# Banks, buffers and ranks: late units of w3 @ w_out in the transposes' banks, score banks kept by the two-branch block, logits behind the first expert product

## The chip, the cores and the metric

The kernel runs on one core of one Trainium2 chip. The metric is the device time of one execution in microseconds (us), as the median of repeated runs. TensorE (PE) does the matmuls and transposes, VectorE (DVE), ScalarE (ACT) and GpSimd (POOL) the element-wise work, and the queue of SyncE (SP) issues almost all DMAs. Each engine takes its instructions in the order of its own program.

## The reference, cut to what matters

```
# 1. attention, 2 batches x 8 heads, 576 positions, head size 64, rotary q and k
attn = softmax(rotate(q) @ rotate(k).T / 8);  x = (attn @ v) laid out as 1152 x 512
# 2. two-branch block
h = ((x @ w1) * (x @ w2)) @ w3                # w1, w2: 512 x 1024, w3: 1024 x 1024
x = h @ w_out                                 # w_out: 1024 x 512
# 3. eight experts, mixed by a gate that is normalised 8 times over rows and columns
P = sinkhorn(exp(x @ w_gate - max))           # 1152 x 8
out = sum_e P[:, e] * (relu(x @ w1e[e]) @ w2e[e])
```

All arrays come as 32-bit or 64-bit floats. Every product is made of three matmuls on pairs (high part, low part) of 32-bit numbers.

## The kernel before, in words

**Stage 1, attention.** The 8 pairs of heads (index n) are worked off tile by tile: five query tiles a pair, the fifth a mixed one. For a tile, PE makes scores into a two-bank PSUM tile of the pool psS (two slots); DVE takes the row maxima (row_max, L371); ACT takes the exponentials (L375); PE transposes them into banks of psT (two slots, L389); ACT or DVE moves them to SBUF (L408); PE multiplies with v into the one bank of psX (values, L446). Keys and queries are rotated on POOL or DVE and spread by DMAs from SBUF to SBUF (kk and sq, L302 to L312).

**Beside it, w3 @ w_out.** The block's last two matrices are multiplied with each other first (w34, 8 row units i). Their 64-bit words come in through two slots of a tile called wide and are turned into a high and a low part by a chain (wide_parts, L174): ACT scales (cvy, L184), DVE shifts, signs and joins in the buffer cvu (L189, L192, L197; two buffers), ACT rounds the high part (L202), POOL or DVE subtracts to get the low part (L205). A unit i takes two pieces u = 2i, 2i+1 of w3, each with four products of three matmuls on all 512 columns (L232 to L234), into one bank; then ACT and DVE split the sum (w34_hi L239, w34_lo L244). w3 has two slots for its pieces, so that piece u+2 is written once the products of u are through. The one bank of psW serves units 0 to 5, a psT bank unit 6 (LATE = 6), and unit 7 (NEARLY) is computed after the stage.

**The order of stage 1 is written out by a planner** (class Plan, L53). Every step has a cost on its engine, the steps that it needs, the slots that it takes and frees, and a rank; whenever an engine is free the step with the lowest rank that can start is next. SIGNAL holds the assumed time from the end of a step to its use on another engine; for a DMA (sp) it is 2.0 beside the time of moving. Where the plan has PE idle before the first step of w34, small matmuls on the identity fill the gap (L623). Ranks of pair n start from t = 18 n: scores at r = t + 3.6 i + j, row_max at r + 0.3, transposes at r + 3.6, values 3.4 tiles after the normalisation's rank; piece u of w3 has 50 + 4.5 u. The products of w34 have ranks above 1000: they run when nothing else can.

**Stage 2, the two-branch block.** Here and later the compiler's scheduler orders the instructions. The pools psS, psT, psX and psW are closed together, and a pool ps of eight banks is opened (four called u, four called z; L629 to L631). Unit 7 of w34 comes first. Then for each of 8 blocks f (columns of w1 and w2, two pieces each through the same wide_parts chain, w12_unit) four branches run, 320, 256, 320 and 256 tokens wide: 12 matmuls into bank pa, 12 into pb (three, L146 to L148), ACT copies pa (a, L664), DVE multiplies it with pb (gf, L666), ACT and DVE split the result (L140, L141). Below, branch k is the k-th of the 32; f = k // 4. merge then multiplies with w34, 4 products a call, in banks u (k = 0) or z (k = 1).

**Stage 3, gate and experts.** All eight banks change hands again (pool pp). logits makes x @ w_gate for the two halves of the tokens (L883), then the experts' products run to the end (hidden, project), with PE almost without a gap.

Of the kernel before, what the change touches and what calls it, by code (L numbers as in the profile page):

```python
# [10 lines left out]
F32 = mybir.dt.float32  # L11
# [7 lines left out]
P = 128  # L19
# [22 lines left out]
WU = 512  # L42
NEARLY = 7
LATE = 6
NSTEP = 2 * E
# [7 lines left out]
class Plan:  # L53
# [4 lines left out]

    SIGNAL = dict(pe=0.28, act=0.14, dve=0.1, pool=0.12, sp=2.0)

# [61 lines left out]
def attention_two_moes(ctx: ExitStack, tc: tile.TileContext, rope, qk, v, mw12, mw3t, mwo, wg, ew1, ew2, out):  # L122
# [20 lines left out]
    def three(ps, terms):  # L143
# [14 lines left out]
    att_p = att.enter_context(sb("att"))  # L158
    psS, psT, psX, psW = (
        aps.enter_context(tc.tile_pool(name=n, bufs=k, space=PSUM)) for n, k in (("psS", 2), ("psT", 2), ("psX", 1), ("psW", 1))  # L160
    )
# [12 lines left out]
    def wide_parts(t, h, l):  # L174

        low, high = t[:, :, 0], t[:, :, 1]
        y = u = None

        def scaled():
            nonlocal y
            y = cv_p.tile([P, WU], F32, name="cvy", bufs=2)
            act.activation(y, f32(high), AF.Copy, scale=2.0**-112)  # L184

        def low_bits():
            nonlocal u
            u = cv_p.tile([P, WU], I32, name="cvu", bufs=2)
            dve.tensor_scalar(u, low, 29, None, op0=ALU.logical_shift_right)  # L189

        def signed():
            dve.scalar_tensor_tensor(  # L192
                out=u, in0=high, scalar=-(2**31), in1=u, op0=ALU.bitwise_and, op1=ALU.bitwise_or
            )

        def joined():
            dve.scalar_tensor_tensor(  # L197
                out=u, in0=y.bitcast(I32), scalar=3, in1=u, op0=ALU.logical_shift_left, op1=ALU.bitwise_or
            )

        def hi_part():
            act.copy(h, f32(u))  # L202

        def lo_part(eng=pool):
            eng.tensor_sub(l, f32(u), f32(h))  # L205

        return scaled, low_bits, signed, joined, hi_part, lo_part
# [17 lines left out]
    def w34_product(u, j, ps_pool, name):  # L225

        i, k = u // 2, u % 2 * 4 + j
        if k == 0:
            w34[i] = ps_pool.tile([P, DM], F32, name=name)
        (h, l, _), (oh, ol, _) = w3[u], wo[k]  # L230
        c = slice(j * P, (j + 1) * P)
        pe.matmul(w34[i], h[:, c], oh, start=(k == 0), stop=False)  # L232
        pe.matmul(w34[i], h[:, c], ol, start=False, stop=False)
        pe.matmul(w34[i], l[:, c], oh, start=False, stop=(k == KF - 1))  # L234
# [184 lines left out]
    def norm_spread(n, g):  # L419

        k = 4 + g
        st["rb", n, g] = rb = att_p.tile([P, 5, D], F32, name="rb", bufs=2)
        act.copy(rb[:, :k], st["sm", n, g][:, :k].unsqueeze(2).to_broadcast([P, k, D]))
# [46 lines left out]

    plan = Plan(psW=1, psX=1, psS=2, psT=2, wide=2, cvy=2, cvu=2, w3=2, raw=2, sq=2, kk=2, v=2, e=2, nm=4, sm=3, rb=2, et0=1, et1=1, r=2, xs=1)

# [14 lines left out]
    for n in range(NP):  # L487
# [33 lines left out]
        for i in range(NQ):  # L521
            g, k, _ = group(i)
            r = t + i * TILE
            for j in range(2 - (i == MIX)):
# [15 lines left out]
                before = [made]  # L540
                step(row_max, (n, i, j), {"dve": 0.68}, r + 0.3, before)
                fr = [("psS", (n, i, j))] + [("nm", (n, i))] * (j or i == MIX)
                step(exponentials, (n, i, j), {"act": 0.73}, r, [(row_max, n, i, j)], frees=fr)
            r += TILE
            parts = 3 - (i == MIX)
# [6 lines left out]
        for g, tiles in enumerate(TILES):  # L552
# [7 lines left out]
            step(norm_moved, a, {"act": act_ps(ng)}, r, [(norm_columns, *a)], [("r", a)], [("psT", (*a, "r"))])  # L560
            r += 3.4 * TILE
            for m, blocks in enumerate(VPARTS):
# [30 lines left out]
    for u in range(2 * KF):  # L593
        i = u // 2
        wide_steps(w3_load, u, w3, 50.0 + 4.5 * u, [("w3", u)])
        if i == NEARLY:
            continue
        for j in range(4):
            needs = [(wo_load, u % 2 * 4 + j, 5), (w3_load, u, 5)]
            needs += [(w34_product, u, j - 1)] if j else [(w34_product, u - 1, 3)] if u else []  # L600
            bank = "psT" if i >= LATE else "psW"
            place = (psT, "t") if i >= LATE else (psW, "w34")
# [26 lines left out]
    aps.close()  # L629
    ps_x = ExitStack()  # L630
    ps_p = ps_x.enter_context(tc.tile_pool(name="ps", bufs=4, space=PSUM))  # L631
# [22 lines left out]
    def branch(f, b, c):  # L654
        wh, wl = w12[f]
        n = CN[c]
        ts = slice(c * CN[0], c * CN[0] + n)
        pa = ps_p.tile([P, 512], F32, name="u")
        pb = ps_p.tile([P, 512], F32, name="u")
        for i, ps in enumerate((pa, pb)):  # L660
# [11 lines left out]
    def merge(c, k):  # L672
# [5 lines left out]
        def product(i, b):  # L678
            ps[i, b] = t = ps_p.tile([P, 512], F32, name="uz"[k])
            ds = slice((2 * i + k) * P, (2 * i + k + 1) * P)  # L680
            bs = slice(b * n, (b + 1) * n)
            three(t[:, :n], [(w34[f][0][:, ds], w34[f][1][:, ds], G[c][:, f, 0, bs], G[c][:, f, 1, bs]) for f in range(KF)])
            return t[:, :n]
# [62 lines left out]
    for u in (2 * NEARLY, 2 * NEARLY + 1):  # L746
        for j in range(4):
            w34_product(u, j, ps_p, "u")
    w34_hi(NEARLY)
# [164 lines left out]
    logits(0)  # L914
    logits(1)
    for k, (c, u) in enumerate(((0, 0), (1, 0), (0, 1), (1, 1))):
        for i, _ in enumerate(hidden(0, c, u)):
            if i == 2 and k == 0:
                gate_start()
# [95 lines left out]
```

## Time and profile before

| | us |
|---|---|
| median of 3 runs (lowest to highest) | 1167.29 (1166.98 to 1168.81) |
| the profiled execution | 1167.42 |
| its span, first to last instruction | 1165.1 |
| PE busy | 1138.6 (98%) |
| DVE busy | 717.8 (62%) |
| ACT busy | 425.5 (37%) |
| POOL busy | 207.3 (18%) |
| mean granted TensorE clock | 0.995 of full speed |

A matmul's row shows a duration that overlaps the next one's, so that the distance between starts is the measure of its cost. "Idle before" is the time in which the engine stood still ahead of an instruction, and the arrow names what ended it. The stages end at about 204 us (attention), 340 us (branches), 391 us (merges).

### The profile page before, as it was taken

The page shows a single profiled execution, that of the slowest core. Times are in us where ns is not written, and L with a number is a line of the kernel's source. Part 1 is how long each engine was busy: PE and PEld are TensorE (multiplying, and loading weights), DVE is VectorE, ACT ScalarE, POOL GpSimd, SP SyncE. Part 2 cuts the span into 40 slices and gives each one's busy share as a digit, 9 for nine tenths or more (in the row PEclk, how much of TensorE's full clock was granted, in tenths as well). Part 3 has the DMA queues.
Part 4 walks back from the last instruction along what each step waited for, and adds up shares of the span by engine and source line. Part 5 has one row for each costly group of instructions (what it writes and reads, how often), then busy time and mean ns, then how long its engine had stood idle before and what let it go on. Part 6 is the DMA issues. An engine that isn't in the chain of part 4 may idle for free.

```text
span 1165.1 us, 17715 instructions
## 1 busy us (share of the span) xinstructions
PE 1138.6 (98%) x7072; PEld 1010.2 (87%) x7072; DVE 717.8 (62%) x1327; ACT 425.5 (37%) x909; POOL 207.3 (18%) x207
## 2 busy tenths in 40 slices
PE   9999999899999999999999999999999999999998
PEld 7867767689999889889889898898988989889887
DVE  6777886796333595565656556566655565655643
ACT  5767666454332343222323232232322232232311
POOL 4475431242000010110211202012011121110200
PEclk9989999999999999999999999999999999999999
DMA  6767771452100021110211101111111111110102
GB/s 214 215 192 211 189 188 37 139 165 78 37 19 1 19 73 37 37 54 20 73 37 37 55 24 68 37 37 55 39 53 39 35 58 52 37 55 19 37 10 73
DMA packets 29153, 83.07 MB, mean 71 GB/s; under 512 B 4880, under 2 KB 6416, under 8 KB 29072
## 3 DMA queue, kind: packets, MB, share of 16 engines
q1 hardware_dynamic: 28528, 81.36, 22.4%
q8 instruction: 55, 0.90, 0.3%
q10 hardware_dynamic: 544, 0.59, 0.2%
q14 instruction: 26, 0.21, 0.1%
HBM read 67.19 MB, written 2.36 MB: 60 GB/s over the span
## 4 chain that ended last, share of the span: by engine, by line
PE 86%; DVE 6%; DMA 3%; ACT 1%; issue 1%; POOL 1%; SPq 1%; DVEq 0%; POOLq 0%; ACTq 0%
PE z L846 12%; PE z L845 11%; PE z L847 11%; PE T L804 4%; PE T L805 4%; PE T L806 4%; PE u L146 3%; PE u L148 3%; PE u L147 3%; PE Q L806 3%; PE Q L804 3%; PE Q L805 3%; PE A L806 3%; PE A L805 3%; PE A L804 3%; PE x L446 2%
## 5 line engine op out<-in xcount | busy, mean ns | idle before, releaser
L847 PE MATMUL z<-w,h 128*128 128x512 f32 x576 | 226.3, 393 | 0.0
L854 DVE SCALAR_TENSOR_TENSOR acc<-z,pr,acc 128x512 f32<-128x512 f32 x135 | 100.9, 748 | 56.6 <-PE z L847 56.5
L847 PEld LDWEIGHTS z<-w,h 128*128 128x128 f32 x576 | 108.0, 187 | 25.3 <-DVE h L811 0.2
L846 PE MATMUL z<-w,y 128*128 128x512 f32 x320 | 126.4, 395 | 0.0
L845 PE MATMUL z<-w,y 128*128 128x512 f32 x320 | 126.3, 395 | 0.0
L724 POOL TENSOR_TENSOR sums<-wide 128x256 f32<-128x256 f32 x28 | 23.7, 848 | 574.5 <-DVE w L141 359.8
L846 PE MATMUL z<-w,h 128*128 128x512 f32 x256 | 101.6, 397 | 0.0
L845 PE MATMUL z<-w,h 128*128 128x512 f32 x256 | 100.8, 394 | 0.0
L140 ACT CAST w<-wide 128x768 fp32r<-128x768 f32 (+1 forms) x64 | 60.4, 943 | 93.2 <-PE z L846 65.0
L810 ACT ACTIVATE y<-tmp 128x320 fp32r<-128x320 f32 x96 | 45.2, 470 | 113.8 <-DVE tmp L826 62.2
L810 ACT ACTIVATE h<-tmp 128x256 fp32r<-128x256 f32 x96 | 40.0, 416 | 127.4 <-DVE tmp L826 120.8
L141 DVE TENSOR_TENSOR w<-wide,w 128x768 fp32r<-128x768 f32 (+1 forms) x64 | 69.6, 1088 | 26.5 <-PE T L806 14.8
L146 PE MATMUL u<-x,w 128*128 128x320 f32 (+1 forms) x256 | 76.4, 298 | 2.6 <-DVE gf L666 2.4
L148 PE MATMUL u<-x,w 128*128 128x320 f32 (+1 forms) x256 | 75.7, 296 | 0.0
L147 PE MATMUL u<-x,w 128*128 128x320 f32 (+1 forms) x256 | 75.4, 295 | 0.0
L846 PEld LDWEIGHTS z<-w,y 128*128 128x128 f32 x320 | 60.7, 190 | 5.7
L845 PEld LDWEIGHTS z<-w,y 128*128 128x128 f32 x320 | 60.2, 188 | 6.0
L811 DVE SCALAR_TENSOR_TENSOR h<-tmp,y 128x320 fp32r<-128x320 f32 x96 | 47.4, 494 | 26.0 <-ACT y L810 25.8
L375 ACT ACTIVATE e<-s,nm 128x576 f32<-128x576 f32 x72 | 53.3, 742 | 18.4 <-DVE nm L371 17.9
L804 PE MATMUL T<-x,w 128*128 128x320 f32 x192 | 59.9, 312 | 0.0
L805 PE MATMUL T<-x,w 128*128 128x320 f32 x192 | 59.2, 309 | 0.0
L806 PE MATMUL T<-x,w 128*128 128x320 f32 x192 | 59.0, 308 | 0.0
(225 smaller groups left out, 3009.5 us busy)
## 6 DMA issues: line engine op xcount, KB each, us to landing
wide<-in_ew_dram SPq DMA_DIRECT2D x64, 512.0 KB, 3.5
wide<-in_mw3t_dram SPq DMA_DIRECT2D x16, 512.0 KB, 4.4
wide<-in_mw_dram SPq DMA_DIRECT2D x16, 512.0 KB, 3.6
raw<-in_qk_dram SPq DMA_DIRECT2D x14, 576.0 KB, 5.4
kk<-raw SPq DMA_DIRECT2D x56, 144.0 KB, 3.1
wide<-in_mwo_dram SPq DMA_DIRECT2D x8, 512.0 KB, 6.7
v<-in_v_dram SPq DMA_DIRECT2D x8, 320.0 KB, 4.1
out_dram<-acc SPq DMA_DIRECT2D x8, 256.0 KB, 2.0
```

Of the source, the lines that this page charges most:

```text
L141: dve.tensor_sub(lo, src, f32(hi))
L146: pe.matmul(ps, wh, xh, start=(i == 0), stop=False)
L147: pe.matmul(ps, wh, xl, start=False, stop=False)
L148: pe.matmul(ps, wl, xh, start=False, stop=(i == n - 1))
L804: pe.matmul(ps, h[:, ws], x[0], start=(first and k == 0), stop=False, **kw)
L805: pe.matmul(ps, h[:, ws], x[1], start=False, stop=False, **kw)
L806: pe.matmul(ps, l[:, ws], x[0], start=False, stop=(k == 1), **kw)
L810: act.activation(h, src, AF.Relu)
L845: pe.matmul(ps, hh[:, f, ts], wh, start=(f == 0), stop=False)
L846: pe.matmul(ps, hh[:, f, ts], wl, start=False, stop=False)
L847: pe.matmul(ps, hl[:, f, ts], wh, start=False, stop=(f == FT - 1))
L854: dve.scalar_tensor_tensor(out=acc[t], in0=ps, scalar=p, in1=acc[t], op0=ALU.mult, op1=ALU.add)
```

## The change

LATE becomes 5: units 5 and 6 of w34 are accumulated in the two psT banks, and unit 5 only starts behind the last transposes of the last pair. psS isn't closed with the other attention pools but lives to the end of stage 2; unit 7 and the branches take its two-bank tiles, pa and pb as the halves of one tile, and so do the products of merge with k = 0 (two pairs a call). The pool ps keeps the four z banks. The conversion buffer cvu has three buffers in place of two; rb, the spread row sums, one in place of two. In the planner: the assumed signal time of a DMA goes from 2.0 to 2.6, row_max from r + 0.3 to r - 0.1, transposes from r + 3.6 to r + 6.0, values from 3.4 to 1.1 tiles behind, piece u of w3 from 50 + 4.5 u to 50 + 7.8 u. In stage 3 logits(1) is issued behind the first product of hidden(0, 0, 0).

```diff
--- before.py
+++ after.py
@@ -41,7 +41,7 @@
 NTT = NT // P
 WU = 512
 NEARLY = 7
-LATE = 6
+LATE = 5
 NSTEP = 2 * E
 FT = F // 2 // P
 
@@ -56,7 +56,7 @@
 
 
 
-    SIGNAL = dict(pe=0.28, act=0.14, dve=0.1, pool=0.12, sp=2.0)
+    SIGNAL = dict(pe=0.28, act=0.14, dve=0.1, pool=0.12, sp=2.6)
 
     SLACK = 0.15
 
@@ -156,8 +156,10 @@
     cv_p = blk.enter_context(sb("cv", side="right"))
     aps, att = ExitStack(), ExitStack()
     att_p = att.enter_context(sb("att"))
-    psS, psT, psX, psW = (
-        aps.enter_context(tc.tile_pool(name=n, bufs=k, space=PSUM)) for n, k in (("psS", 2), ("psT", 2), ("psX", 1), ("psW", 1))
+    ps_x = ExitStack()
+    psS = ps_x.enter_context(tc.tile_pool(name="psS", bufs=2, space=PSUM))
+    psT, psX, psW = (
+        aps.enter_context(tc.tile_pool(name=n, bufs=k, space=PSUM)) for n, k in (("psT", 2), ("psX", 1), ("psW", 1))
     )
 
     YW = 2 * KF * CB[1]
@@ -185,7 +187,7 @@
 
         def low_bits():
             nonlocal u
-            u = cv_p.tile([P, WU], I32, name="cvu", bufs=2)
+            u = cv_p.tile([P, WU], I32, name="cvu", bufs=3)
             dve.tensor_scalar(u, low, 29, None, op0=ALU.logical_shift_right)
 
         def signed():
@@ -226,7 +228,8 @@
 
         i, k = u // 2, u % 2 * 4 + j
         if k == 0:
-            w34[i] = ps_pool.tile([P, DM], F32, name=name)
+            t = ps_pool.tile([P, 2, 512] if name == "s" else [P, 512], F32, name=name)
+            w34[i] = t[:, 0] if name == "s" else t
         (h, l, _), (oh, ol, _) = w3[u], wo[k]
         c = slice(j * P, (j + 1) * P)
         pe.matmul(w34[i], h[:, c], oh, start=(k == 0), stop=False)
@@ -419,7 +422,7 @@
     def norm_spread(n, g):
 
         k = 4 + g
-        st["rb", n, g] = rb = att_p.tile([P, 5, D], F32, name="rb", bufs=2)
+        st["rb", n, g] = rb = att_p.tile([P, 5, D], F32, name="rb", bufs=1)
         act.copy(rb[:, :k], st["sm", n, g][:, :k].unsqueeze(2).to_broadcast([P, k, D]))
 
     def norm_columns(n, g):
@@ -468,7 +471,7 @@
         x, h, l = x_parts(n, g)
         eng.tensor_sub(l, x, f32(h))
 
-    plan = Plan(psW=1, psX=1, psS=2, psT=2, wide=2, cvy=2, cvu=2, w3=2, raw=2, sq=2, kk=2, v=2, e=2, nm=4, sm=3, rb=2, et0=1, et1=1, r=2, xs=1)
+    plan = Plan(psW=1, psX=1, psS=2, psT=2, wide=2, cvy=2, cvu=3, w3=2, raw=2, sq=2, kk=2, v=2, e=2, nm=4, sm=3, rb=1, et0=1, et1=1, r=2, xs=1)
 
     def step(f, args, costs, rank, needs=(), takes=(), frees=(), **kw):
 
@@ -538,10 +541,10 @@
                         needs = needs + [(mix_first, 0), (mix_first, 1)]
                     step(mixed_scores, (n,), {"pe": 1.14 if n else 1.7}, r + j, needs, tk, fr)
                 before = [made]
-                step(row_max, (n, i, j), {"dve": 0.68}, r + 0.3, before)
+                step(row_max, (n, i, j), {"dve": 0.68}, r - 0.1, before)
                 fr = [("psS", (n, i, j))] + [("nm", (n, i))] * (j or i == MIX)
                 step(exponentials, (n, i, j), {"act": 0.73}, r, [(row_max, n, i, j)], frees=fr)
-            r += TILE
+            r += 6.0
             parts = 3 - (i == MIX)
             for p in range(parts):
                 needs = [(exponentials, n, i, min(p, 1) * (i < MIX))] + ([(transposes, n, i, p - 1)] if p else [(transposes, n, i - 1, 0)] if k else [])
@@ -558,7 +561,7 @@
             step(norm_spread, a, {"act": act_sb((4 + g) * D)}, r, [(norm_rows, *a)], [("rb", a)], [("sm", a)])
             step(norm_columns, a, {"pe": (0.24, 0.4)[g]}, r, [(norm_spread, *a)], [("psT", (*a, "r"))], [("rb", a)])
             step(norm_moved, a, {"act": act_ps(ng)}, r, [(norm_columns, *a)], [("r", a)], [("psT", (*a, "r"))])
-            r += 3.4 * TILE
+            r += 1.1 * TILE
             for m, blocks in enumerate(VPARTS):
                 parts = {(i, p) for i in tiles for t in blocks for p in (({0, 2}, {1})[t > 2] if i < MIX else {int(t > 2)})}
                 needs = [(moved, n, i, p) for i, p in sorted(parts)] + [(load_v, n)]
@@ -592,12 +595,14 @@
         wide_steps(wo_load, j, wo, 12.0 + 5.9 * j, [])
     for u in range(2 * KF):
         i = u // 2
-        wide_steps(w3_load, u, w3, 50.0 + 4.5 * u, [("w3", u)])
+        wide_steps(w3_load, u, w3, 50.0 + 7.8 * u, [("w3", u)])
         if i == NEARLY:
             continue
         for j in range(4):
             needs = [(wo_load, u % 2 * 4 + j, 5), (w3_load, u, 5)]
             needs += [(w34_product, u, j - 1)] if j else [(w34_product, u - 1, 3)] if u else []
+            if i == LATE and u % 2 == j == 0:
+                needs.append((transposes, NP - 1, MIX, 1))
             bank = "psT" if i >= LATE else "psW"
             place = (psT, "t") if i >= LATE else (psW, "w34")
             plan.step(
@@ -627,7 +632,6 @@
 
 
     aps.close()
-    ps_x = ExitStack()
     ps_p = ps_x.enter_context(tc.tile_pool(name="ps", bufs=4, space=PSUM))
     g_p = blk.enter_context(sb("g", side="right"))
 
@@ -655,8 +659,8 @@
         wh, wl = w12[f]
         n = CN[c]
         ts = slice(c * CN[0], c * CN[0] + n)
-        pa = ps_p.tile([P, 512], F32, name="u")
-        pb = ps_p.tile([P, 512], F32, name="u")
+        both = psS.tile([P, 2, 512], F32, name="s")
+        pa, pb = both[:, 0], both[:, 1]
         for i, ps in enumerate((pa, pb)):
             ws = [slice((i * KD + d) * P, (i * KD + d + 1) * P) for d in range(KD)]
             three(ps[:, :n], [(wh[:, ws[d]], wl[:, ws[d]], X[b][:, 2 * d, ts], X[b][:, 2 * d + 1, ts]) for d in range(KD)])
@@ -676,7 +680,12 @@
         ps = {}
 
         def product(i, b):
-            ps[i, b] = t = ps_p.tile([P, 512], F32, name="uz"[k])
+            if k:
+                t = ps_p.tile([P, 512], F32, name="z")
+            else:
+                if (i, b) in ((0, 0), (1, 1)):
+                    ps[i] = psS.tile([P, 2, 512], F32, name="s")
+                t = ps[i][:, b]
             ds = slice((2 * i + k) * P, (2 * i + k + 1) * P)
             bs = slice(b * n, (b + 1) * n)
             three(t[:, :n], [(w34[f][0][:, ds], w34[f][1][:, ds], G[c][:, f, 0, bs], G[c][:, f, 1, bs]) for f in range(KF)])
@@ -745,7 +754,7 @@
     w12_unit(0)
     for u in (2 * NEARLY, 2 * NEARLY + 1):
         for j in range(4):
-            w34_product(u, j, ps_p, "u")
+            w34_product(u, j, psS, "s")
     w34_hi(NEARLY)
     w34_lo(NEARLY)
     for f in range(KF):
@@ -912,9 +921,10 @@
 
     prepare_first(0, 1)
     logits(0)
-    logits(1)
     for k, (c, u) in enumerate(((0, 0), (1, 0), (0, 1), (1, 1))):
         for i, _ in enumerate(hidden(0, c, u)):
+            if i == 0 and k == 0:
+                logits(1)
             if i == 2 and k == 0:
                 gate_start()
             if i == 4 or (i == 1 and k):
```

## Rows read from the trace of the kernel before

**Rows 1.** The page's busy times, and PE's clock in 40 equal slices (tenths).
```profile
PE 1138.6 (98%) x7072; PEld 1010.2 (87%) x7072; DVE 717.8 (62%) x1327; ACT 425.5 (37%) x909; POOL 207.3 (18%) x207
...
PEclk9989999999999999999999999999999999999999
```

**Rows 2.** Windows: us, busy time by engine, granted clock, DMA share, GB/s.
```profile
75.00:90.00 15.00, 12.99 (x76) 8.79 (x75) 8.49 (x12) 7.55 (x18) 12.33 (x7) 0.77 0.64 193
...
226.00:230.00 4.00, 3.90 (x10) 3.14 (x11) 3.25 (x5) 1.70 (x4) 1.86 (x2) 0.57 0.34 120
...
240.00:250.00 10.00, 9.04 (x66) 8.78 (x66) 9.72 (x14) 5.41 (x13) 5.16 (x4) 1.00 0.53 188
```

**Rows 3.** PE's waits, whole span: total us, times, longest.
```profile
PE t L389 <- ACT e L375: 4.6, 6, 1.4
PE s L341 <- DMA sq<-raw: 3.2, 2, 1.9
PE w L232 <- DVE keep L244: 3.1, 3, 1.5
PE u L146 <- DVE gf L666: 2.4, 4, 1.0
```

**Rows 4.** PE's timeline, first matmuls of w34's units 4, 5, 7 and branch 0.
```profile
203.95 0.39 PE L234 MATMUL w<-y 128*128 128x512 f32 x1
205.81 0.50 PE L232 MATMUL w<-y 128*128 128x512 f32 x1 [1.47 <-DVE keep L244]
...
212.95 0.50 PE L232 MATMUL w<-y 128*128 128x512 f32 x1 [1.40 <-DVE keep L244]
...
226.10 0.80 PE L232 MATMUL u<-y 128*128 128x512 f32 x1 [1.98 <-DVE keep L244]
...
233.28 0.31 PE L146 MATMUL u<-x,w 128*128 128x320 f32 x1
```

**Rows 5.** POOL's timeline, the last low part of w12's first block.
```profile
230.40 1.48 POOL L205 TENSOR_TENSOR w<-cvu,w 128x512 fp32r<-128x512 f32 x1 [2.54 <-ACT w L202]
```

**Rows 6.** DVE's timeline, three starts of a conversion (L189).
```profile
226.66 1.48 DVE L189 TENSOR_SCALAR cvu<-wide 128x512 int32<-128x512 int32 x1 [0.61 <-POOL y L205]
...
279.20 1.50 DVE L189 TENSOR_SCALAR cvu<-wide 128x512 int32<-128x512 int32 x1 [1.34 <-POOL w L205]
...
281.56 0.41 DVE L189 TENSOR_SCALAR cvu<-wide 128x512 int32<-128x512 int32 x1
```

**Rows 7.** PE's timeline in the branches: starts of pa or pb.
```profile
246.09 0.31 PE L146 MATMUL u<-x,w 128*128 128x320 f32 x1
...
248.97 0.41 PE L146 MATMUL u<-x,w 128*128 128x320 f32 x1 [0.96 <-DVE gf L666]
...
257.03 0.41 PE L146 MATMUL u<-x,w 128*128 128x320 f32 x1 [0.65 <-DVE gf L666]
...
271.11 0.41 PE L146 MATMUL u<-x,w 128*128 128x320 f32 x1 [0.34 <-DVE gf L666]
```

**Rows 8.** DVE's timeline, two of the products gf.
```profile
248.44 0.48 DVE L666 TENSOR_TENSOR gf<-u,a 128x320 f32<-128x320 f32 x1
...
283.10 0.48 DVE L666 TENSOR_TENSOR gf<-u,a 128x320 f32<-128x320 f32 x1
```

**Rows 9.** PE's timeline at the first logits.
```profile
392.65 3.08 PE L883 MATMUL z<-x,wgs 128*16 128x320 f32 x20 [1.47 <-DVE y L141]
```

**Rows 10.** DVE's timeline, the last two splits of the merges.
```profile
392.08 0.42 DVE L141 TENSOR_TENSOR y<-z,y 128x256 fp32r<-128x256 f32 x1 [0.44 <-ACT y L140]
392.42 0.41 DVE L141 TENSOR_TENSOR y<-f,y 128x256 fp32r<-128x256 f32 x1
```

**Rows 11.** DMA issues: count, KB each, median us from issue to landing.
```profile
kk<-raw SPq DMA_DIRECT2D x56, 144.0 KB, 3.1
...
sq<-raw SPq DMA_DIRECT2D x14, 144.0 KB, 4.1
```

**Rows 12.** Windows of L623 alone, 0 to 220 us: the sum.
```profile
sum 220.00, PE 25.98 PEld 23.58; mean PE 2.36 PEld 2.14
```

## The prediction

> **What bounds the kernel now.** The busy times come first: PE is busy for 98% of the span, and no other engine comes near [rows 1]. So a change can only save what PE wastes: time in which it stands still, runs at a low clock, or runs fillers. The slices of the clock show where: two dips only, both in the first fifth [rows 1]. The windows put them at 75 to 90 us (granted clock 0.77) and 226 to 230 us (0.57), a mixture of the levels 2.4 and 1.2 GHz [rows 2]. The list of PE's waits then names the stops: 4.6 us for exponentials, 3.2 us for spread queries, 3.1 us for the split of a w34 unit and 2.4 us for the products gf [rows 3]. All lie ahead of 280 us; from there to the end only the logits' wait of 1.47 us is worth a row [rows 9]. The fillers cost 26.0 us [rows 12]; they only take time that PE could not use, and half of them are the start-up. So the argument is about the first 280 us: the attention, the units of w34 behind it (204 to 233 us), and the first dozen branches (233 to 276 us).
>
> **Unit boundaries (LATE, psS kept).** Unit 4 starts 1.47 us late, unit 5 1.40 us, unit 7 1.98 us, each time because the bank's last reader, the low split on DVE, has to finish first [rows 4]. Unit 6 had a bank of its own and shows no wait. Two units with that one wait take 226.10 - 1.98 - 212.95 = 11.2 us, or about 5.5 us each; unit 7 takes 233.28 - 226.10 = 7.2 us, so 1.7 us go to the half clock that follows its wait [rows 2, 4]. In the new kernel unit 5 finds a free psT bank, unit 6 the other, and unit 7 a score bank that the last exponentials left long ago. Unit 4 still follows unit 3 in psW, so I leave its 1.47 us in place. The gain at PE is 1.40 + 1.98 + 1.7 = 5.1 us.
>
> What is late next are the weights of the first branch. Their last low part is ready at 230.40 + 1.48 = 231.9 us [rows 5], 1.4 us before PE needs it; PE would now come at 233.28 - 5.1 = 228.2 us. The conversions move forward too: the last pieces of w3 wait for products of earlier units, which come 1.40 us sooner, and the third cvu buffer takes away the 0.61 us for which DVE waited for POOL at 226.66 and the 1.48 - 0.41 = 1.07 us by which that instruction was longer than a free one [rows 6]. That is 3.1 us: weights at 228.8 us. From there on DVE carries the conversions of the next blocks with 9.72 of 10 us busy [rows 2], so what is handed on is the smaller of PE's and DVE's lead: 3.1 us. Bounds: 0 (weights and DVE don't move) to 5.1.
>
> **pa and pb as one tile.** Before, a branch could start its 12 matmuls of pa once ACT had copied the pa of two branches earlier, and waited for the product gf only ahead of pb. As one tile it can't start before that gf has ended. The 12 matmuls of pa ran from 246.09 to 248.01 (248.97 less its wait of 0.96), some 1.76 us by their starts [rows 7]. The gf that ends at 248.44 + 0.48 = 248.92 would now hold up branch 4 at its start, from 246.1 to 249.0: 2.9 us of wait for 0.96. It isn't 1.76 us each time, since a late branch finds the next gf done. Walking branches 4 to 14 along DVE's times as they stand, with 3.53 us for a wide branch (twice 1.76) and 2.82 us for a narrow one (256 columns for 320): 4 ends at 252.5 (was 250.8), 6 at 260.6 (was 258.9), 8 at 267.3 (was 266.0), 10 at 274.6 (was 273.0), and 14, which now waits for the gf ending at 283.6 [rows 8], at 287.4 (was 285.9). So the cost settles at +1.5 us. Bounds: 0, if DVE's lead shortens its lag, and 4 x 1.76 = 7.0 us, if each of the four waits [rows 3] costs its pa in full. I take +1.5. Behind branch 16 the conversions are over and gf follows its branch at once, so there the pairs cost nothing, and the merges find their banks free.
>
> **Third cvu buffer, later blocks.** At 279.20 DVE had waited 1.34 us for POOL's low part to free a buffer, and the gf at 283.10 is queued behind that conversion [rows 6, 8], and once a block this comes again. A pause of this kind cost PE 0.34 us at 271.11 [rows 7]. I take -0.5 for two blocks; bounds 0 and -2.7 (the wait of 1.34 us in full, twice). Set against it: the conversion that started as POOL ran its next low part took 1.50 us, a free one 0.41 [rows 6]. The Trainium skill (SBUF — State Buffer, Who interferes with whom) says that the two engines share a pair of SBUF ports, which whoever issues first holds for the whole instruction, while a tensor_scalar in its two-port mode is fully blocked. By that rule, with which these rows agree, an earlier start beside POOL buys nothing: the 1.07 us above and this 0.5 us drop out, and the sum would be 1164.3.
>
> **The plan of the attention.** The trace has no row for the new order, so only bounds can be given. For: the assumed 2.0 us of a DMA plus 0.6 us of moving stand against measured landings of 3.1 us for keys and 4.1 us for queries [rows 11]; PE twice stood waiting for such a landing, 3.2 us [rows 3], and the first stop lies in the window with clock 0.77, where 0.46 of 15 us at half clock is some 3.4 us of lost work [rows 2]. With 2.6 the plan puts other work or fillers there. Row maxima ahead of moves, scores two tiles ahead of transposes, and values before the transposes that need their slot should feed ACT sooner, against the 4.6 us for exponentials. The most to gain is 3.2 + 4.6 = 7.8 us, and 3.4 more for the clock. Against: pieces of w3 come later, and PE's gaps between 95 and 204 us are filled by just these products (units 0 to 3). A unit that isn't ready moves 5.5 us behind the attention. Rows exist for the waits and none for late pieces, since two w3 slots held these back anyway; so I take a third of 7.8, -2.6. rb with one slot is used twice a pair and its two steps are short; I take nothing, and a wait would come within the same bounds.
>
> **Logits.** PE waits 1.47 us until 392.65, just behind the end of a split at 392.08 + 0.42 = 392.50 [rows 9, 10]. These first matmuls belong to logits(0), whose inputs were ready long before. That split is the last reader of a z bank, so what they wait for is a bank of the new pool, not logits(1)'s data. Unit 7 at 226.10 shows the same: the first tile of a new pool waits for the last reader of the old one [rows 4]. Moving logits(1) behind the expert's first product leaves this wait in place: 0, bounds 0 and -1.5. No DMA is moved by it, and its four copies on ACT only queue behind one more.
>
> **Sum.** 1167.4 (profiled; the median is 0.1 lower) - 3.1 + 1.5 - 0.5 - 2.6 + 0 = 1162.7 us.
>
> **Rivals.** *The pairs cost more than the banks give* (slower). Speaks for it: DVE at 97% in 240 to 250 us, so that gf lags. Price 7.0 - 3.1: 1171.3. It decides once each gf ends more than 1.76 us after the branch before it is through; ahead of branch 4 it is 2.8 us late, ahead of branch 10 about 2.2 (271.11 less 0.34 and less the 1.92 us of pa gives 268.9), in between less [rows 7]. Chance 0.12. *Late w3 pieces* (slower): one unit of 5.5 us is pushed behind the attention, 3.1 gained: 1169.8. Against it: before, the pieces were ready ahead of their use. Chance 0.08. *The lead is eaten up* (no change): PE arrives early, waits for w12's weights and pays for the pairs, the plan gives nothing: 1167.4 - 0.6 - 0.5 + 1.5, about 1167.5. Chance 0.20. *The plan gives all of it* (faster still): -7.8 in place of -2.6, and 1.5 for the logits: 1156.0. Chance 0.15. The forecast keeps 0.45.
>
> **How the numbers follow.** Within 0.2% (2.3 us) this measurement can't tell a change from none. Faster: 0.45 + 0.15 = 0.60; same 0.20; slower 0.12 + 0.08 = 0.20. The range takes in the larger gain and the smaller of the slower cases: 1156 to 1170. The likeliest case's own range is 1159 to 1165.
>
> **What would show it.** Right: no wait of w34 products for the split at units 5 and 7, full clock from 220 to 235 us, the wait of branch 4 or its like now ahead of pa and longer; the end of the attention at 200 to 203 us; a wait of about 1.5 us still ahead of the first logits. Wrong: pauses of PE in the attention for exponentials or w3 parts longer than the 4.6 us of before, more than four w34 units left at its end, or waits for gf beyond 6 us in total.

## The result and the profile after

The kernel after takes 1152.38 us in the median of 4 runs (1151.36 to 1154.34), the kernel before 1167.85 beside it: ratio 0.9881 [0.9865, 0.9897]. The two medians lie 15.5 us apart; the ratio alone would make it 13.9 us (0.0119 of 1167.85). Below, differences are those of the medians. The forecast of 1162.7 had the direction right and a third of the size, and the time lies below its range.

The page of the kernel after, busy time of each engine and slices of TensorE's clock:

```profile
PE 1128.7 (98%) x7074; PEld 1008.5 (88%) x7074; DVE 718.1 (62%) x1334; ACT 426.2 (37%) x907; POOL 198.3 (17%) x202
...
PEclk9999999999999999999999999999999999999999
```

The slices of before show one dip, the third slice [rows 1]; the low clock at 226 to 230 us that the prediction counts as a second one is seen only in its window [rows 2]. In the slices of after no dip is left, but a finer window still has one, smaller than the 0.77 of before, in the place where PE waits for a move on DVE (window: length, busy time of PE, PEld, DVE, ACT and POOL with instructions, granted clock, DMA share, GB/s):

```profile
75.00:90.00 15.00, 12.61 (x91) 10.74 (x90) 13.45 (x17) 9.89 (x25) 7.96 (x5) 0.89 0.67 185
83.75 0.90 PE L392 MATMUL t<-ident,e 128*128 128x128 f32 x3 [2.39 <-DVE et L411]
```

Three marks of the order, by source line, say in which stage the time went: the values' products (the last ends the attention), the first matmul of branch 0, and its last one (start of the first, start of the last, behind the minimum, median and maximum duration in ns). Line numbers of the kernel after run up to 9 higher (L449 is the old L446, L670 the old L666, L892 the old L883). Before, then after:

```profile
L446 PE MATMUL x<-et,v x320: 379/432/796, 23.2 to 203.0; 128*64 128x256 f32 x80, 128*64 128x320 f32 x80
L146 PE MATMUL u<-x,w x256: 278/308/419, 233.3 to 339.7; 128*128 128x320 f32 x64, 128*128 128x256 f32 x64
```

```profile
L449 PE MATMUL x<-et,v x320: 379/431/484, 23.7 to 191.2; 128*64 128x256 f32 x80, 128*64 128x320 f32 x80
L146 PE MATMUL s<-x,w x256: 278/308/417, 212.1 to 323.5; 128*128 128x320 f32 x64, 128*128 128x256 f32 x64
```

The values end 11.8 us sooner (203.0, 191.2), the first branch starts 21.2 us sooner (233.3, 212.1), and the branches give back 5.0 us of it (106.8 from the first branch to the first merge, then 111.8). From the first merge to the end it is 825.0 us before and 825.6 after. So the attention and the units behind it gave all, and the branches took some back.

PE's waits in the kernel after, whole span (total us, times, longest), which answer to [rows 3]:

```profile
PE s L146 <- DVE gf L670: 5.6, 4, 1.5
PE t L392 <- DVE et L411: 2.4, 1, 2.4
PE s L146 <- DVE keep L247: 2.3, 1, 2.3
...
PE z L892 <- DVE y L141: 1.5, 1, 1.5
PE s L344 <- DMA sq<-raw: 1.4, 2, 1.0
PE s L237 <- POOL y L207: 1.0, 1, 1.0
```

Gone are the exponentials and the splits at the unit boundaries; the spread queries fell from 3.2 to 1.4 us; the products gf rose from 2.4 to 5.6, the branches have a wait that they did not have (keep, 2.3), and one transpose waits 2.4 us for DVE's move (et).

### The profile page after: what moved, and what is told of

Same layout as the page of the kernel before. It is cut to its first block, busy times and chain, and to the rows that moved or that the text cites. A ratio compares the mean times of both kernels' runs of the same rounds, so it can differ in the third digit from the quotient of the medians.

```text
span 1149.5 us, 17646 instructions
## 1 busy us (share of the span) xinstructions
PE 1128.7 (98%) x7074; PEld 1008.5 (88%) x7074; DVE 718.1 (62%) x1334; ACT 426.2 (37%) x907; POOL 198.3 (17%) x202
## 4 chain that ended last, share of the span: by engine, by line
PE 92%; DVE 5%; DMA 1%; issue 1%; POOL 0%; ACT 0%; DVEq 0%; POOLq 0%; ACTq 0%; SPq 0%
PE z L855 12%; PE z L854 12%; PE z L856 12%; PE T L813 4%; PE T L814 4%; PE T L815 4%; PE s L344 3%; PE x L449 3%; PE s L146 3%; PE s L148 3%; PE s L147 3%; PE Q L815 3%; PE Q L813 3%; PE Q L814 3%; PE A L815 3%; PE A L814 3%
## 5 line engine op out<-in xcount | busy, mean ns | idle before, releaser
L146 PE MATMUL s<-x,w 128*128 128x320 f32 (+1 forms) x256 | 76.2, 298 | 7.9 <-DVE gf L670 5.6
L148 PE MATMUL s<-x,w 128*128 128x320 f32 (+1 forms) x256 | 75.6, 295 | 0.0
L147 PE MATMUL s<-x,w 128*128 128x320 f32 (+1 forms) x256 | 75.4, 294 | 0.0
L374 DVE TENSOR_REDUCE nm<-s 128x1 f32<-128x576 f32 x72 | 52.4, 751 | 11.2 <-PE s L344 7.4
```

Of the source, the lines that this page charges most:

```text
L146: pe.matmul(ps, wh, xh, start=(i == 0), stop=False)
L147: pe.matmul(ps, wh, xl, start=False, stop=False)
L148: pe.matmul(ps, wl, xh, start=False, stop=(i == n - 1))
```

## The experiments

Each time below stands against the kernel before on the same chip, whose median moved between 1166.1 and 1167.9. "PE stands" is the stretch from 20 us to the first matmul of branch 0 less PE's busy time in it, in the one profiled execution; that execution can lie some microseconds off its kernel's median: the runs of w3_sp scatter by 12.5 us, and those of the kernel before, 19 of them on one chip, by 15.2.

R, W and S are the three groups of numbers of the plan:

```diff
-SIGNAL = dict(pe=0.28, act=0.14, dve=0.1, pool=0.12, sp=2.0)              # S
+SIGNAL = dict(pe=0.28, act=0.14, dve=0.1, pool=0.12, sp=2.6)
-step(row_max, (n, i, j), {"dve": 0.68}, r + 0.3, before)                  # R
+step(row_max, (n, i, j), {"dve": 0.68}, r - 0.1, before)
-r += TILE                      (transposes)                               # R
+r += 6.0
-r += 3.4 * TILE                (values)                                   # R
+r += 1.1 * TILE
-wide_steps(w3_load, u, w3, 50.0 + 4.5 * u, [("w3", u)])                   # W
+wide_steps(w3_load, u, w3, 50.0 + 7.8 * u, [("w3", u)])
```

| kernel | median us | ratio [95%] | against before, us | PE stands, us | clock from 20 us | first branch at |
|---|---|---|---|---|---|---|
| before | 1167.29 | | | 15.1 | 0.98 | 233.3 |
| R alone (e1_ranks) | 1169.65 | 1.0024 [1.001, 1.0038] | +3.3 | 20.1 | 0.97 | 233.4 |
| W alone (e2_w3rank) | 1163.29 | 0.9976 [0.9952, 0.9999] | -3.1 | 11.8 | 0.99 | 224.3 |
| S alone (e3_sp) | 1164.37 | 0.9987 [0.996, 1.0014] | -2.0 | 16.0 | 0.95 | 236.5 |
| W and S (w3_sp) | 1166.83 | 1.0002 [0.9972, 1.0032] | +0.3 | 14.9 | 0.99 | 227.1 |
| R and S (ranks_sp) | 1159.13 | 0.9937 [0.9915, 0.9958] | -7.4 | 10.5 | 0.97 | 223.2 |
| R and W (ranks_w3) | 1157.80 | 0.993 [0.9907, 0.9954] | -8.7 | 14.1 | 0.99 | 222.0 |
| R, W and S (plan) | 1151.89 | 0.9873 [0.9855, 0.9892] | -14.3 | 5.8 | 1.00 | 214.3 |
| plan, row_max at r + 0.3 (p_row) | 1162.66 | 0.9964 [0.9949, 0.9978] | -4.8 | 13.6 | 0.98 | 227.4 |
| plan, transposes by TILE (p_tr) | 1161.24 | 0.9956 [0.9927, 0.9986] | -6.2 | 13.1 | 0.95 | 234.0 |
| plan, values by 3.4 TILE (p_val) | 1151.67 | 0.9877 [0.9851, 0.9902] | -15.8 | 9.3 | 1.00 | 216.5 |
| before, row_max at r - 40 (row_first) | 1159.60 | 0.9928 [0.9906, 0.995] | -8.2 | 11.4 | 0.98 | 224.9 |
| plan, row_max at r - 40 (row_first_plan) | 1165.44 | 0.998 [0.9962, 0.9998] | -2.3 | 13.2 | 0.98 | 228.9 |
| plan, cvu 3, rb 1 (plan_cvu) | 1153.18 | 0.9886 [0.9866, 0.9906] | -13.0 | 12.7 | 0.98 | 223.8 |
| banks alone (e4_banks) | 1168.57 | 1.0019 [1.0003, 1.0035] | +2.2 | 12.2 | 0.99 | 226.6 |
| after | 1152.38 | 0.9881 [0.9865, 0.9897] | -15.5 | 5.0 | 0.99 | 212.1 |

**One group alone, and the banks alone.** R, W and S by themselves, and a kernel with LATE = 5, psS kept and pa and pb as one tile, cvu and the plan's numbers as before:

> The kernel before with the three ranks of the attention alone: row maxima at r - 0.1, transposes at r + 6.0, values 1.1 tiles behind. If the order of scores, transposes and values is what shortened the attention (theory R), most of the 11.8 us by which the last values end earlier (191.6 for 203.4 us) appear here: the last values end by 195 us and the time is 1155 to 1160. If the gain is the later pieces of w3 (theory W) or the longer assumed DMA time (theory D), the attention ends at 201 to 205 us and the time stays within 3 us of before.

> The kernel before with the ranks of the pieces of w3 alone, 50 + 7.8 u. Theory W (conversions with better ranks held up the attention's row maxima and moves on DVE): the attention ends 6 us or more earlier and the time is 1158 to 1162. Theories R and D: within 3 us of before, or up to 5.5 us slower, if a unit of w34 is left over behind the attention.

> The kernel before with the assumed DMA time alone, 2.6 for 2.0. Theory D: PE's 3.2 us of waits for spread queries shrink to below 1 us, the window 75 to 90 us keeps its full clock, and the time falls by 3 to 6 us. Theories R and W: within 3 us of before.

> The kernel before with the banks alone: LATE = 5 with its wait for the last transposes, psS kept, pa and pb as one tile, unit 7 in a score bank; two cvu buffers, old ranks. The attention should end at 203 us as before. My step: the two waits of 1.40 and 1.98 us and 1.7 us of low clock go, the weights of the first branch come late, and the pairs cost 1.5 us, together -1 to -3 us. Rival (pairs eat it up): waits for gf of 5 us and more, time within 1 us of before or slower.

No group of numbers gives more than 3.1 us alone. The banks alone measured 1168.57, ratio 1.0019 [1.0003, 1.0035], 2.2 us slower. The interval of S takes in no change at all. None of the four parts gives even a third of the 15.5 us, so either they act together or the third cvu buffer, not yet tested here, carries the gain; the next pair of runs decides. Of the expected marks, W's attention ended 6.6 us earlier as foreseen (196.4 for 203.0), with a time just above its range; R ended its attention at 220.2 us, in neither of its ranges; S stayed within 3 us, as the theories against it say, though its own step came partly true: the waits for spread queries fell from 3.2 to 1.3 us and the clock from 75 to 90 us rose to 1.00, while over the whole stretch the clock came out lower, 0.95 for 0.98; e4_banks went the rival's way, with waits for gf of 6.7 us.

**The plan as a whole, and with the third cvu buffer.** plan has R, W and S with all banks and buffers as before; plan_cvu adds cvu with 3 buffers and rb with 1.

> The kernel before with the three changes of the plan's numbers together (ranks of the attention, ranks of w3's pieces, DMA time 2.6), old banks, two cvu buffers. Alone they gave +0.2%, -0.2% and -0.1%. If they work only together (theory T: each takes away what the other would wait for), the first branch starts by 222 us (before: 233.3) and the time is 1152 to 1158. If the buffers or the banks carry the gain (theory B), the first branch starts at 228 us or later and the time is 1160 to 1168.

> The same with the third cvu buffer and the single rb. Theory B (the third buffer lets the conversions run beside the low part on POOL all through the attention): 5 us or more faster than without, the first branch by 219 us. Theory T: within 3 us of the run without it.

The plan alone gives 14.3 us, as good as all of the change, with the first branch at 214.3 us as theory T has it. With the third buffer 1153.18, 0.9886 [0.9866, 0.9906]: the intervals lie over each other, and the buffer brings nothing that can be measured. The marks of the two profiled executions differ far more than that (first branch at 214.3 and 223.8 us), but these executions took 1149.53 and 1155.84 us, the fastest and the slowest of their four, and the branches of plan_cvu took 105.2 us for 108.4; so such a mark is known to some microseconds only.

**Groups in pairs.**

> The kernel before with w3's later pieces and the DMA time of 2.6, but the old ranks in the attention. Theory T1 (the attention's own ranks are needed, since they decide what PE and DVE do when the pieces come later): not faster than 1160. Theory T2 (the pair w3 and DMA time carries the gain, the attention's ranks add little): 1152 to 1156.

> The kernel before with the attention's ranks and the DMA time of 2.6, but w3's pieces at 50 + 4.5 u. If early pieces of w3 are what spoils the new ranks (row maxima and moves on DVE behind conversions), 1164 or more. If the DMA time mends them, below 1160.

> The kernel before with the attention's ranks and w3's later pieces, but the DMA time of 2.0. If the ranks and the pieces make the gain between them, 1152 to 1157. If the plan still has PE stand before late DMAs, waits for keys, queries and loads of 3 us and more and 1160 or more.

Any single group taken out of the plan costs 5.6 us (S), 6.9 (W) or 14.6 (R), though alone they gave -2.0, -3.1 and +3.3: the effects of these numbers don't add. W and S without R came out as T1 said. R and S fell below 1160, the case in which the DMA time mends the new ranks. R and W lie 0.8 us above the range in which they make the gain by themselves, and 5.9 above the plan.

**One rank at a time taken back.**

> The kernel with the three changes of the plan's numbers (0.9873 of before), but row maxima back at r + 0.3. If the row maxima's rank is what takes them out from behind the conversions on DVE (ACT waited 17.9 us for them before), ACT's wait for row maxima is back above 10 us and the time at 1160 or more. If 0.4 of a rank changes little, within 3 us of 1152.

> The same, but transposes and moves back at r + 3.6. If it is the scores two tiles ahead of the transposes that keep ACT fed, PE's and ACT's waits for one another come back and the time is 1159 or more; otherwise within 3 us of 1152.

> The same, but values back at 3.4 tiles behind. If the old rank held the next pair's transposes up (they take the slots that values free), waits of PE's transposes for their slots and 1158 or more; otherwise within 3 us of 1152.

The row maxima's rank and the transposes' rank are each worth 8 to 10 us within the plan (14.3 less 4.8, and less 6.2); that of the values nothing. All three came out on the side that their expectation gives for it (p_row: ACT's wait 10.4 us and 1162.66). That a rank moved by 0.4 costs 9.5 us leaves a rival that no run tests: that part of the 14.3 us belongs to this one order and not to later pieces or a longer DMA time as such. It would take a set of orders with numbers close to the plan's.

**Row maxima first.** In the trace of before ACT stands still for row maxima while DVE converts; the next test gives them a rank ahead of every conversion, once in the order of before and once in the plan.

```diff
-step(row_max, (n, i, j), {"dve": 0.68}, r + 0.3, before)
+step(row_max, (n, i, j), {"dve": 0.68}, r - 40.0, before)
```

> The kernel before with one number changed: row maxima at r - 40, ahead of everything else on DVE. If ACT's wait for row maxima behind conversions (17.4 us from 20 to 205 us) is what paces the old attention, this alone makes a good part of the gain: the wait below 8 us and 1154 to 1162. If the new order as a whole is needed, so that PE has the next scores ready as well, the wait shrinks but the time stays within 4 us of before.

> The three changes of the plan's numbers with row maxima at r - 40 in place of r - 0.1. If they are out of the conversions' way at r - 0.1 already, 1150 to 1155 as with it; if conversions in front of them still cost time there (7.2 us of waits are left), 1146 to 1150.

This one number gave 8.2 us in the order of before and took 12.0 from the plan. The first time lies in its expected range, but the wait that was to bring it did not fall below 8 us; the second fits neither expectation. ACT's waits for row maxima from 20 to 205 us, in before, plan, row_first and row_first_plan in this order:

```profile
ACT e L375 <- DVE nm L371: 17.4, 17, 5.2
```

```profile
ACT e L375 <- DVE nm L371: 7.2, 12, 1.6
```

```profile
ACT e L375 <- DVE nm L371: 13.2, 17, 1.6
```

```profile
ACT e L375 <- DVE nm L371: 17.0, 13, 4.2
```

Where the row maxima were put ahead of everything in the plan, ACT waited for them more, not less: the list scheduler answers one number with another order as a whole. Nor does this wait set the time alone: w3_sp has 10.9 us of it and is no faster than before, the kernel after has 9.9.

**The banks on top of the plan.** a_four is the kernel after with four pairs for the branches: the wide ones keep psS, the narrow ones take two z banks. best is a_four with the low parts of w12's blocks 5 to 7 on DVE in place of POOL.

```diff
-both = psS.tile([P, 2, 512], F32, name="s")
-pa, pb = both[:, 0], both[:, 1]
+if c:
+    pa, pb = (ps_p.tile([P, 512], F32, name="z") for _ in range(2))
+else:
+    both = psS.tile([P, 2, 512], F32, name="s")
+    pa, pb = both[:, 0], both[:, 1]
...
-wide_split(wide_load(mw12[f, x]), h[:, r], l[:, r])          # best only
+wide_split(wide_load(mw12[f, x]), h[:, r], l[:, r], dve if f > 4 else pool)
```

> The changed kernel with more banks in the branches: the narrow branches (256 columns) take two of the four z banks, which stand empty until the merges, and only the wide ones a score pair, so that a branch follows the fourth before it in its banks and not the second. If the pairs' waits for gf (5.6 us) and for unit 7's split (2.3 us) are what the branches lose (111.8 us from the first branch to the first merge, before 106.8), they go: 104 to 106 us, time 1144 to 1148. Rival: DVE, 96% busy from 220 to 240 us, sets the pace, and the wait comes back as one for weights: 110 us and more, time within 2 us of the changed kernel.

> The changed kernel with four bank pairs in the branches, as in the run before, and the low parts of w12's last three blocks on DVE in place of POOL. There DVE stood 2.56 us for POOL's low part at 249 us, the gf behind it came late, PE waited 2.35 us and had half clock after it. If that was POOL's doing: the wait goes, 2 to 4 us less, 1144 to 1146. Rival: the high part on ACT is what comes late, so the wait stays: 1147 to 1149.

a_four measured 1147.68, 0.9842 [0.9825, 0.986]; best 1143.28, 0.9799 [0.9772, 0.9826], both faster than the kernels before and after. From the first branch to the first merge it is 106.8 us in before, 111.8 in after, 107.1 in a_four, 103.3 in best. The times are at or below the expected ranges, the stretch of a_four 1.1 us above its own. What is left of PE's waits in the branches (5.6 for gf and 2.3 for unit 7's split in the kernel after, above), in a_four, then in best:

```profile
PE s L146 <- DVE gf L673: 2.6, 2, 2.3
```

```profile
PE s L146 <- DVE gf L675: 0.4, 2, 0.2
```

The rival that DVE sets the pace does not hold: in a_four DVE is just as busy in these branches, 9.54 of 10 us, and PE does not stand there.

```profile
222.00:232.00 10.00, 10.00 (x78) 10.00 (x77) 9.54 (x15) 5.69 (x12) 4.51 (x3) 1.00 0.49 156
```

**Logits in the old place.** a_nolog is the kernel after with logits(1) straight behind logits(0).

> The changed kernel with logits(1) in its old place, ahead of the expert's first product. My step: the wait of 1.5 us ahead of the first logits is one for a bank of the new pool and stays in either place; within 0.5 us of the changed kernel. Rival: the moved product covers a wait, 1.0 to 1.5 us slower than the changed kernel.

1153.69, 0.9886 [0.9869, 0.9902] against 0.9881. The medians lie 1.3 us apart, which would suit the rival, but the intervals are too wide to tell. The traces settle it: the first logits wait 1.5 us in both, and from the first merge to the end, where the move acts, both take 825.6 us. The move is worth nothing.

## Why the prediction was wrong, step by step

**The plan of the attention: the step that failed.** It stood with "a third of 7.8, -2.6" and measured -14.3. The waits were named rightly (exponentials, spread queries, a low clock ahead of 90 us); the size was not. Two windows, from 20 us to the first branch, before and plan (length, PE busy and instructions, granted clock, DMA share, GB/s):

```profile
20.00:233.28 213.28, 198.20 (x1341) 0.98 0.58 165
```

```profile
20.00:214.30 194.30, 188.52 (x1329) 1.00 0.62 179
```

PE stood still for 213.28 - 198.20 = 15.1 us before and for 194.30 - 188.52 = 5.8 in the plan: 9.3 us. The waits for exponentials before, from 20 us on:

```profile
PE t L389 <- ACT e L375: 3.7, 5, 1.4
PE s L341 <- ACT e L375: 1.1, 1, 1.1
PE t L392 <- ACT e L375: 0.3, 1, 0.3
```

All of PE's waits that are left in the plan:

```profile
PE u L232 <- DVE keep L244: 2.0, 1, 2.0
PE w L232 <- DVE keep L244: 1.7, 2, 1.4
PE s L341 <- DMA sq<-raw: 1.3, 2, 1.0
PE t L392 <- ACT e L375: 0.3, 1, 0.3
PE s L341 <- ACT e L375: 0.3, 1, 0.3
```

Of the waits named in the prediction, those for exponentials almost all went (5.1 us before, 0.6 here), those for spread queries by more than half (3.2, 1.3). These two give 6.4 of the 9.3 us; the rest are one less wait for a split and a handful of short ones that the prediction left out. The clock gave its share: it was 0.77 in 75 to 90 us and 0.57 in 226 to 230 us [rows 2], 0.23 x 15 + 0.43 x 4 = 5.2 us of lost work, and is 1.00 in every window of the plan from 20 us to its first branch. So the term of -2.6 was too small by 11.7 us, and even its bound of 7.8 + 3.4 lies 3.1 us below the 14.3. Taking a third of it had no row behind it, the clock's 3.4 us were named and then not put into the sum at all, and the short waits were left out. The rival that the plan gives all of it (1156.0, chance 0.15) came nearest, and was still 3.6 us too slow.

Of the 19.0 us between the two marks, 9.3 are standing and 5.2 clock; another 1.6 or so are six products of the first pair that come ahead of 20 us (1.0) and four fillers fewer in the stretch (90, 86). The 3 us that are left lie in PE's busy time, and no row that was read says what they are; this execution of plan is also 2.4 us faster than its median.

The argument against the gain, that later pieces of w3 starve PE, did not come true. From 100 to 180 us, before, then after:

```profile
100.00:180.00 80.00, 74.06 (x520) 56.12 (x521) 61.78 (x98) 56.39 (x142) 36.89 (x22) 1.00 0.65 177
```

```profile
100.00:180.00 80.00, 80.00 (x576) 64.07 (x576) 69.95 (x122) 62.24 (x153) 35.19 (x24) 1.00 0.61 175
```

PE never stands there in the kernel after and makes 576 matmuls in place of 520; DVE does 122 instructions for 98. DVE had time left, but at the wrong moments. One such moment in before, on DVE, then ACT (start, duration):

```profile
153.98 3.17 DVE L192 SCALAR_TENSOR_TENSOR cvu<-wide,cvu 128x512 int32<-128x512 int32 x1
157.19 1.78 DVE L197 SCALAR_TENSOR_TENSOR cvu<-cvy,cvu 128x512 int32<-128x512 int32 x1
158.90 1.41 DVE L371 TENSOR_REDUCE nm<-s 128x1 f32<-128x576 f32 x2
```

```profile
159.68 0.74 ACT L375 ACTIVATE e<-s,nm 128x576 f32<-128x576 f32 x1 [5.17 <-DVE nm L371]
```

ACT stands 5.17 us while DVE, in its fixed order, first converts a piece of w3 (and is held up in that itself, see the last section). Summed, ACT waited 17.4 us for row maxima in the attention, and the prediction never looked at ACT's or DVE's waits: it asked what PE's few listed stops could give, not how many steps upstream had been late to make them. That moving the row maxima alone gives 8.2 us (row_first) shows that their place in the order matters; that this wait is the cause is not shown, since it only fell from 17.4 to 13.2 us there, and w3_sp, with 10.9, gained nothing. What is shown is that R, W and S together bring the gain, and that it comes as PE's standing time and clock in the attention. Which step of the order makes R, W and S worth 14.3 us together and next to nothing apart stays open.

**Unit boundaries: right, and the doubt about it wrong.** PE around units 5, 6 and 7 in the kernel after (start, duration; idle before in brackets), which answers to [rows 4]:

```profile
194.23 0.39 PE L237 MATMUL w<-y 128*128 128x512 f32 x1
194.46 0.39 PE L235 MATMUL t<-y 128*128 128x512 f32 x1
...
205.11 0.39 PE L237 MATMUL t<-y 128*128 128x512 f32 x1
205.34 0.39 PE L235 MATMUL s<-y 128*128 128x512 f32 x1
...
209.70 0.50 PE L237 MATMUL s<-y 128*128 128x512 f32 x1 [0.98 <-POOL y L207]
212.11 0.31 PE L146 MATMUL s<-x,w 128*128 128x320 f32 x1
```

Units 5 and 7 begin 0.23 us behind the product before them, without a wait for a split, at full clock (1.00 from 200 to 240 us in the windows). The one stop left is for a low part of w3. With the banks alone (e4_banks) the first branch starts at 226.6 for 233.3: 6.7 us, of which 1.1 are the attention's (values end at 201.9 for 203.0); the tail gives 5.6, against 5.1 foreseen at PE. On top of the plan it is much the same: from the last values to the first branch 26.2 us in plan (188.1 to 214.3) and 28.1 in plan_cvu, against 20.9 in the kernel after and 20.5 in a_nolog. But I let only 3.1 of it through, for w12's weights that would be late. They hardly were: in e4_banks the first branch waits once, for a low part, and in the kernel after not at all.

```profile
PE s L148 <- POOL w L207: 0.3, 1, 0.3
```

That the conversions came forward with the products that free their buffers would explain it; no run tests that alone. Nor does a wait ahead of unit 7 always bring a low clock: in plan unit 7 still waits 1.98 us, and the clock stays at 1.00 up to the first branch. So the plan won the 1.7 us of half clock without the banks.

**pa and pb as one tile: right in kind, too small.** +1.5 foreseen, bounds 0 to 7.0. It cost 5.0 in the kernel after (106.8, 111.8) and 7.6 in e4_banks (114.4). The same stretch takes 105.2 us in plan_cvu and 108.4 in plan, both with the old banks, and 114.8 in a_nolog with the pairs, so the cost is known to some 3 us at best. The stops, in the kernel after, answering to [rows 7]:

```profile
218.12 0.39 PE L146 MATMUL s<-x,w 128*128 128x256 f32 x1 [2.33 <-DVE keep L247]
222.68 0.41 PE L146 MATMUL s<-x,w 128*128 128x320 f32 x1 [1.41 <-DVE gf L670]
231.00 0.41 PE L146 MATMUL s<-x,w 128*128 128x320 f32 x1 [1.46 <-DVE gf L670]
238.93 0.41 PE L146 MATMUL s<-x,w 128*128 128x320 f32 x1 [1.28 <-DVE gf L670]
253.39 0.42 PE L146 MATMUL s<-x,w 128*128 128x320 f32 x1 [1.42 <-DVE gf L670]
```

The first is one I had not seen: unit 7 sits in one of the two pairs, so branch 1 waits for unit 7's split. The others hold up whole branches, ahead of pa, as foreseen; but I had reckoned that a branch once late finds the next gf done, so that the cost settles. DVE is 19.13 of 20 us busy from 220 to 240, its conversions come forward with PE's start, and it lags again at branches 2, 4, 6 and 10. a_four shows that it is the number of pairs: with four, the 5.0 us are gone (107.1 against 106.8). So in e4_banks 6.7 won and 7.6 lost make 0.9 us slower in the marks, 2.2 in the medians; on top of the plan 0.9881 against plan_cvu's 0.9886, nothing that can be measured. The rival that the pairs cost more than the banks give was right about this part of the change, and the plan covered it.

**Third cvu buffer: -0.5, measured nothing.** 0.9886 with it against 0.9873 without, intervals of 0.2% on each side; a half microsecond either way could not be seen. The single rb was changed in the same run and taken as nothing in the prediction; the two are not told apart.

**Logits: right.** No gain was foreseen and none came. The wait stays, at the same place, for a split that reads the bank, answering to [rows 9]:

```profile
377.04 3.08 PE L892 MATMUL z<-x,wgs 128*16 128x320 f32 x20 [1.47 <-DVE y L141]
379.96 0.31 PE L813 MATMUL A<-x,w 128*128 128x320 f32 x1
380.84 2.52 PE L892 MATMUL z<-y,wgs 128*16 128x256 f32 x20
```

**Signs and sums.** Of the signs of being right, all came true but one: the attention ended at 191.2 us and not at 200 to 203, which points at the failed step. No sign of being wrong came, as they were all drawn up for a loss: no wait for exponentials is left in the list, and the waits for gf add up to 5.6 us. One sum of the rivals is off: 1167.4 - 0.6 - 0.5 + 1.5 is 1167.8, not 1167.5; nothing hangs on it.

## What to carry to other kernels

Where an order is written by a planner, bound a change of its numbers by everything that the bottleneck loses in that stage: here 15.1 us of standing and 5.2 of clock, against 14.3 won and a listed bound of 7.8. Keep both ends of the bound, and don't take a third of it for want of a row. Test such numbers together, since R, W and S were worth +3.3, -3.1 and -2.0 us alone (the last no clear change) and -14.3 as a set. Where two buffers are merged into one that is handed over as a whole, count who else sits in the pool and add slots: two more pairs gave 4.7 us here by the medians (1152.38 to 1147.68; 3.0 when each is set against its own run of the kernel before), and with the low parts of three blocks moved from POOL to DVE it came to 1143.28.

## What the runs showed that I had not expected

The DVE instruction at 153.98 above took 3.17 us, where the median of its 40 likes is 0.69 (0.68 at 280.95, with POOL idle). POOL ran this beside it:

```profile
153.97 2.64 POOL L273 TENSOR_TENSOR raw<-raw,tab 128x1152 f32<-128x1152 f32 x1 [10.97 <-DMA sq<-raw]
156.69 1.74 POOL L277 TENSOR_TENSOR raw<-raw 128x576 f32<-128x576 f32 x1
```

DVE's started 0.01 us later and ended at 157.15, 0.54 us behind the end of POOL's, as if it had stood through nearly all of it. The next pair does the same: DVE's at 157.19 took 1.78 us and ended at 158.97, again 0.54 us behind POOL's, which ran from 156.69 to 158.43. The Trainium skill (SBUF — State Buffer, Who interferes with whom) describes the ports that DVE and GpSimd share as an exclusive lock. These rows agree, with 2.5 and 1.1 us lost. So, as an estimate from these rows, some 3.6 of the 5.17 us for which ACT stood there come from POOL's work beside the conversions and not from their place in DVE's order; a planner's fixed costs don't know of it.
